# Two transformer-like layers on one core: the orders of all five queues and the PSUM banks replaced by newly searched lists

## The chip, the core and the metric

The kernel runs on one core of a Trainium2 chip. The metric is the device time of one execution in microseconds; the median of the timed executions counts. Five engines work side by side, each through a queue of its own in order: TensorE (PE, with its weight loads PEld), VectorE (DVE), ScalarE (ACT), GpSimd (POOL) and SyncE (SP), which here issues all DMAs.

## The reference

Two layers, each a sliding-window attention block and an MLP block on x of 2048 tokens by 576:

```python
def _A_ref(x, wqkv, wo):
    H = 32; Dh = D // H; W = 256
    q, k, v = heads(x @ wqkv)                      # 32 heads of 18
    scores = einsum("bhqd,bhkd->bhqk", q, k) * Dh ** -0.5
    scores = where(0 <= i - j < W, scores, -1e9)   # causal, the last 256 tokens
    return merge(einsum("bhqk,bhkd->bhqd", softmax(scores), v)) @ wo

def _B_ref(x, w1, b1, w2, b2):
    h = gelu(layernorm(x) @ w1 + b1)               # 576 -> 4608
    return h @ w2 + b2

x = x + _A_ref(layernorm(x), wqkv, wo)
x = x + _B_ref(layernorm(x), w1, b1, w2, b2)
x = x + _A_ref(layernorm(x), wqkv, wo)             # the same weights again
x = x + _B_ref(layernorm(x), w1, b1, w2, b2)
```

## The kernel before

The tokens are cut into four chunks of 512 (four tiles of 128), so two layers give eight chunks, numbered 0 to 7 here; 4 to 7 are the second layer. x stays in SBUF in float32. The weights of the MLP don't fit and are streamed again for every chunk.

A chunk passes through these stages. *Normalization*: VectorE's statistics, GpSimd's root, VectorE's scaled copy, and a DMA transpose that SyncE issues. *Queries, keys and values* (`qkv`): per tile six products of 288 columns; VectorE or ScalarE copies them out of PSUM, and a DMA transpose brings queries and keys into the layout for the scores (stage names such as q1.3: chunk 1, tile 3). *Attention* (`E`): the heads form eight groups. For each group TensorE computes scores (`scores` for chunks 0, 1 and 4, `halves` with tiles of 64 columns for the others), ScalarE takes the exponential (`exps`, L978), GpSimd cuts the band's edges (`cut`, L987), and TensorE multiplies with the values (`pv`, L1058; stage names such as ea6.p0); VectorE transposes and normalizes the result. Part a, b and c of a chunk's attention run beside the MLP of the chunk before. *Tail*: the output projection (L1182), the residual, the next normalization. *MLP* in three thirds: an up product with GELU (`G_part`, L1227 and L1237; stages ga, gb, gc) and a down product (`mm2`; stages ma, mb, mc) that adds to the residual through VectorE (L1164).

How TensorE's tasks are built matters for the change. A task is a run of matmuls that is not interrupted, and it has a *mode*, the tiling of the array: "f" whole array, "r" and "q" scores in tiles of 32 rows, "c" tiles of 32 columns, "h" two halves of 64 rows. In mode "h" (the up product, the output projection, and queries, keys and values from chunk 2 on) a product is two tasks on the same two banks: the second one (`own=True`) adds what the other half of the array contributes, and waits until the first has ended. The products in mode "c" can be *narrow* (four matmuls of 32 columns, L843) or *wide* (one of 128 columns, L840), with the same result. `schedule` decides which: where the planner's clock finds that 300 instructions would pass within 5.4 us (`dense`, constants FETCH and FETCH_US), a run of such products is made wide.

The order of the work is written out. The builder makes 4077 tasks with numbers, and `ORDER` lists for each of the five queues the numbers in the order in which that queue runs them; `BANKS` gives the PSUM bank (one of eight) of each of 1149 allocations, in the order of the task numbers. Semaphore waits follow from what tasks read and write. `schedule` runs a planner's clock over the lists with each task's cost only to decide wide or narrow and to put filler matmuls into early gaps. So `"... 768 769 466 ..."` in TensorE's list means: both halves of a product of chunk 2's first tile, then the first scores of chunk 1.

Task numbers used below: 782 to 811 products of chunk 2's tiles (stage q2); 374, 377 product and transpose of the last query tile of chunk 1, 382 the transpose of its last key tile, 466 the scores that need them; 235 and 240 pieces of wo, 328 the broadcast of b2; 413 to 450, 814 to 851, 1341 to 1378, 1868 to 1905, 2301 to 2327 output projections; 1300 to 1341 and 1812 to 1865 products of chunks 3 and 4; 1517, 3124, 3509 products with the values, 3520 scores.

## Time and profile before

| | us |
|---|---|
| median of three timed executions | 861.28 (860.0 to 861.43) |
| profiled execution, its own time | 858.9 |
| span of the profiled execution | 857.2 |
| TensorE busy in it | 843.1 |
| ScalarE busy | 611.2 |
| VectorE busy | 391.0 |
| GpSimd busy | 371.7 |

The span is what the trace covers; 1.7 us lie around it. Matmuls are pipelined and the profile models their ends, so a busy TensorE can contain pauses: they show when the starts of neighbouring rows are compared. A row of the timeline reads: start, length, engine, line, operation, tile written and tiles read, shape, count, and in brackets the idle time before it with what released it. "issue" stands for time in which an engine waited for nothing that the profile shows.

### The profile page before, as it was taken

Reading aid. Unit: us, or ns where it says so; the run is one execution under the profiler, and the core shown is the slowest. Engines: PE = TensorE matmul, PEld = TensorE weight load, DVE = VectorE, ACT = ScalarE, POOL = GpSimd, SP = SyncE. Lnnn points to the kernel's source line nnn. Section 1 sums busy time; section 2 is a strip of 40 time slices with the busy share of each in tenths; the row PEclk is TensorE's granted clock in tenths of the full one; section 3 lists DMA queues with packets and bytes.
Section 4 is the critical chain, followed back from the end, with each engine's and each line's share of the span. In section 5 each row is a group of like instructions: output and inputs, shape, how many; then the busy total and the mean of one; then the engine's idle time right before and its main releaser. Section 6 shows DMA issues by size and latency. Waiting matters only on the chain.

```text
span 857.2 us, 28905 instructions
## 1 busy us (share of the span) xinstructions
PE 843.1 (98%) x12490; PEld 525.2 (61%) x12490; DVE 391.0 (46%) x943; ACT 611.2 (71%) x1052; POOL 371.7 (43%) x551
## 2 busy tenths in 40 slices
PE   9999999999999999999999999999999999999998
PEld 6555655656656566665576665756656666656656
DVE  7877324654228442474354633564224624253103
ACT  5888886878867788488715898548887689962550
POOL 4766734545234644256500493415544266331100
DMA  9796746354475634936277545485527753636510
GB/s 226 128 153 112 219 115 176 79 152 113 141 162 95 176 113 132 192 49 160 88 226 159 116 100 141 93 196 124 169 95 194 159 140 107 206 130 180 184 68 28
DMA packets 181999, 119.91 MB, mean 140 GB/s; under 512 B 107504, under 2 KB 181872, under 8 KB 181872
## 3 DMA queue, kind: packets, MB, share of 16 engines
q1 hardware_dynamic: 181872, 118.05, 55.8%
q8 instruction: 99, 1.62, 0.8%
q14 instruction: 28, 0.23, 0.1%
HBM read 90.10 MB, written 2.36 MB: 108 GB/s over the span
## 4 chain that ended last, share of the span: by engine, by line
PE 93%; ACT 2%; DVE 2%; issue 1%; DMA 1%; POOL 1%; SPq 0%; DVEq 0%
PE ps L1227 33%; PE ps L840 28%; PE ps L905 8%; PE ps L843 7%; PE ps L1058 5%; PE ps L1182 4%; PE ps L1037 4%; PE ps L1002 2%; ACT pT L978 2%; PE ps L859 2%; DMA kT<-qn 1%; POOL pT L987 1%; PE ps L741 0%; DVE oq L1064 0%; DVE xn L780 0%
## 5 line engine op out<-in xcount | busy, mean ns | idle before, releaser
L978 ACT ACTIVATE pT<-ps 128x512 bf16<-128x512 f32 (+5 forms) x692 | 363.7, 638 | 59.6 <-PE ps L1037 38.2
L987 POOL TENSOR_SCALAR_AFFINE_SELECT pT<-pT 128x512 bf16<-128x512 bf16 (+1 forms) x360 | 278.7, 798 | 218.9 <-ACT pT L978 217.4
L1227 PE MATMUL ps<-xnTm,w_sb 64*128 64x512 bf16 x2592 | 293.2, 376 | 1.3 <-DVE x_res L1164 0.4
L1237 ACT ACTIVATE hT<-ps,b1col 128x512 bf16<-128x512 f32 x276 | 169.7, 689 | 145.9 <-PE ps L1227 144.8
L840 PE MATMUL ps<-w_sb,hT 128*128 128x288 bf16 x1674 | 220.0, 287 | 0.8 <-issue 0.7
L1227 PEld LDWEIGHTS ps<-xnTm,w_sb 64*128 64x128 bf16 x2592 | 130.0, 94 | 139.7 <-issue 7.2
L840 PEld LDWEIGHTS ps<-w_sb,hT 128*128 128x128 bf16 x1674 | 156.3, 98 | 52.5 <-issue 11.1
L1164 DVE TENSOR_TENSOR x_res<-ps,x_res 128x288 f32<-128x288 f32 x224 | 98.9, 451 | 187.9 <-PE ps L840 141.2
L905 PE MATMUL ps<-wqkv,xnTa 64*128 64x288 bf16 x1296 | 93.8, 283 | 0.9 <-ACT pT L978 0.2
L885 DVE CAST qn<-ps 128x288 bf16<-128x288 f32 x104 | 44.0, 450 | 106.8 <-PE ps L905 102.1
L905 PEld LDWEIGHTS ps<-wqkv,xnTa 64*128 64x128 bf16 x1296 | 62.5, 94 | 29.8 <-PE ps L905 4.1
L1064 DVE STREAM_TRANSPOSE oq<-ps 128x512 f32<-128x512 f32 x64 | 45.7, 714 | 69.6 <-PE ps L1058 68.8
L764 POOL TENSOR_SCALAR vtmp<-mv_all 128x1 f32<-128x1 f32 (+1 forms) x43 | 10.0, 233 | 147.9 <-DVE mv_all L755 145.8
L843 PE MATMUL ps<-w_sb,hT 128*32 128x288 bf16 x1752 | 61.1, 287 | 0.0
L1242 POOL TENSOR_TENSOR x_res<-x_res,b2bc 128x576 f32<-128x576 f32 x32 | 40.6, 1283 | 34.0 <-ACT hT L1237 33.8
L751 DVE BATCH_NORM_STATS2 st_all<-x_res 128x6 f32<-128x288 f32 (+1 forms) x128 | 52.7, 444 | 3.6 <-DMA x_res<-in_A_x_dram 3.4
L1058 PE MATMUL ps<-pT,vA 128*20 128x384 bf16 (+2 forms) x1440 | 50.9, 273 | 1.6 <-issue 1.3
L885 DVE CAST vA<-ps 128x288 bf16<-128x288 f32 x56 | 24.0, 448 | 60.0 <-PE ps L905 59.3
L843 PEld LDWEIGHTS ps<-w_sb,hT 128*32 128x32 bf16 x1752 | 44.1, 97 | 10.8 <-issue 3.9
L1037 PE MATMUL ps<-qT,kT 32*64 32x256 bf16 (+4 forms) x2080 | 42.7, 252 | 0.8 <-ACT pT L978 0.8
L1182 PE MATMUL ps<-wo_sb,attT 64*128 64x288 bf16 x576 | 42.0, 283 | 0.8
L1058 PEld LDWEIGHTS ps<-pT,vA 128*20 128x20 bf16 x1440 | 29.1, 91 | 18.5 <-issue 5.9
(62 smaller groups left out, 483.6 us busy)
## 6 DMA issues: line engine op xcount, KB each, us to landing
w_sb<-in_B_w_dram SPq DMA_DIRECT2D x46, 864.0 KB, 5.9
w_sb<-in_B_w_dram SPq DMA_DIRECT2D x48, 768.0 KB, 5.4
w_sb<-in_B_w_dram SPq DMA_DIRECT2D x96, 48.0 KB, 3.5
out_dram<-x_res SPq DMA_DIRECT2D x16, 144.0 KB, 2.8
wqkv<-in_A_wqkv_dram SPq DMA_DIRECT2D x3, 576.0 KB, 5.5
x_res<-in_A_x_dram SPq DMA_DIRECT2D x3, 576.0 KB, 4.4
wqkv<-in_B_w_dram SPq DMA_DIRECT2D x2, 864.0 KB, 8.5
wo_sb<-in_A_wo_dram SPq DMA_DIRECT2D x4, 144.0 KB, 2.9
```

Of the source, the lines that this page charges most:

```text
L840: return e.matmul(bank(b)[:, 0:HB], lhs, rhs, start=start, stop=stop, skip_group_check=True)
L843: ins = e.matmul(bank(b)[32 * j:32 * j + 32, 0:HB], lhs[:, 32 * j:32 * j + 32], rhs, start=start, stop=stop, tile_position=(0, 32 * j), sk ...
L885: return e.tensor_copy(dst, src)
L905: ins = e.matmul(bank(bs[o])[:, 0:HB], xnTa[r:r + 64, c, i * 128:(i + 1) * 128], wqkv[r:r + 64, c, col:col + HB], start=(c == 4), stop=(ph ...
L978: add("act", lambda e, h2=h2: e.activation(pT[:, sl, 2 * h2:2 * h2 + 2, dst:dst + n], two(bs[h2])[:, :, src:src + n], ACT.Exp, scale=SCALE ...
L987: add("pool", lambda e: e.affine_select(ap, ap, pattern=pat, compare_op=(ALU.is_ge if kind == "d" else ALU.is_gt), fill=0.0, base=0, chann ...
L1037: ins = e.matmul(two(bs[j // 2])[64 * u:64 * u + 64, j % 2, 64 * col:64 * (col + n)], k_of(T0 + so)[0][32 * j:32 * j + 32, g, 64 * u:64 * ...
L1058: ins = e.matmul(bank(bo)[32 * j:32 * j + VW, qo * 128:(qo + nq) * 128], vA[:, (T0 + so) % VS, 8 * j + g, :], pT[:, sl, j, col:col + nq * ...
L1164: add("dve", lambda e: e.tensor_tensor(x_res[:, t, sl], bank(b)[:, 0:HB], x_old[:, t, sl], ALU.add), reads=[b] + ([f"xin{t}"] if first els ...
L1182: ins = e.matmul(bank(bs[o])[:, 0:HB], attT[r:r + 64, c, i * 128:(i + 1) * 128], wo_sb[r:r + 64, c, o * HB:o * HB + HB], start=(c == 4), s ...
L1227: ins = e.matmul(bank(bks[i])[:, 0:n], w1_sb[r:r + 64, sls[i], col:col + 128], xnTm[r:r + 64, k % 2, c, 0:n], start=(c == 4), stop=(ph == ...
L1237: add("act", lambda e, ff=ff, hd=hd, bk=bk: e.activation(hd[:, 0:n], bank(bk)[:, 0:n], ACT.Gelu_apprx_tanh, bias=b1col[:, ff:ff + 1]), rea ...
```

## The change

The five lists of `ORDER` and the string `BANKS` are replaced: 945 of 1175 places of TensorE's list hold another task, 872 of 1055 of ScalarE's, 784 of 943 of VectorE's, 453 of 547 of GpSimd's, 305 of 357 of SyncE's, and 982 of 1149 bank numbers differ. The tasks are the same. The planner's cost of a `halves` task falls by 0.02 us (HALF_EXTRA), and its costs for VectorE's and ScalarE's copies of the first chunk's products rise to 0.435 and 0.42 us. The lists' lines that the prediction speaks of, and the rest of the diff:

```diff
 PACE = {"f": 16.0, "c": 65.0, "r": 100.0, "h": 18.5, "s": 33.0, "q": 160.0}
-HALF_EXTRA = 0.05
+HALF_EXTRA = 0.03
 FETCH = 300
...
 ORDER = {
     "pe":
...
-        "247 336 384 257 342 227 262 341 266 359 369 252 373 275 374 271 294 360 378 284 379 279 299 365 364 289 370 303 308 "
-        "782 783 758 312 759 772 777 773 778 461 316 768 769 466 763 764 425 426 471 413 414 449 476 450 437 438 485 791 481 "
...
-        "1840 1841 1689 1517 1617 1690 1686 1521 1687 1674 1671 1528 1672 1680 1681 1677 1626 1678 1538 1633 1675 1683 1684 "
...
-        "3163 3004 3096 3159 3171 3015 3172 3160 3153 3154 3105 3168 3169 3025 3112 3165 3166 3150 3128 3151 3124 3135 3186 "
...
-        "3576 3591 3566 3578 3567-3569 3590 3592 3476 3655 3497 3667 3668 3656 3673 3513 3674 3520 3509 3658 3659 3601 3661 "
...
+        "247 331 257 384 227 262 341 342 266 359 252 360 271 275 379 369 284 364 294 373 279 299 365 378 289 370 374 308 312 "
+        "758 782 759 303 783 772 777 773 778 461 316 768 769 466 763 329 764 425 426 471 413 414 449 476 450 437 438 485 786 "
...
+        "1505 1845 1840 1846 1841 1517 1617 1689 1690 1686 1521 1674 1687 1528 1675 1671 1672 1626 1680 1677 1681 1538 1633 "
...
+        "3015 3154 3159 3160 3105 3171 3172 3168 3025 3112 3165 3169 3166 3124 3128 3305 3310 3306 3311 3186 3135 3177 3188 "
...
+        "3569 3566 3578 3568 3579 3590 3592 3476 3497 3655 3667 3668 3656 3673 3513 3674 3658 3520 3509 3659 3676 3601 3661 "
...
     "sp":
...
-        "242 324 325 237 245 403 232 354 236 363 377 368 235 240 328 382 762 767 409 412 424 436 460 448 719 579 578 540 541 "
...
+        "238 235 233 349 403 363 406 368 243 382 377 232 240 781 762 246 767 409 412 245 436 460 424 448 719 328 539 578 540 "
...
 BANKS = (
-        "076102773623254242404063044624420401540205741676503072304020214204145376776476745031236203530030333603112726025527"
...
 
 
 def build_kernel(nc, A_x, A_wqkv, A_wo, B_x, B_w1, B_b1, B_w2, B_b2, out):
@@ -912,7 +912,7 @@
                 for o in range(2):
                     add("dve", lambda e, o=o, b=bs[o]: drain(e, vA[:, sv, o * 16:(o + 1) * 16, 0:DH],
                                                            bank(b)[:, 0:HB].rearrange("p (h d) -> p h d", d=DH)),
-                        reads=[bs[o]] + scale, writes=[f"v{sv}h{o}"], cost=0.375, lat=0.14, prio=prio)
+                        reads=[bs[o]] + scale, writes=[f"v{sv}h{o}"], cost=0.375 if k else 0.435, lat=0.14, prio=prio)
             else:
                 sl = qn_ctr[0] % NQN
                 qn_ctr[0] += 1
@@ -921,10 +921,10 @@
                     dst = qv[:, 2 * o:2 * o + 2, :, 0:DH]
                     if o == 1 and (k == 0 and i < 3 or k == 2):
                         add("act", lambda e, b=bs[o], dst=dst: e.copy(dst, heads_of(bank(b))) if k else e.mul(dst, heads_of(bank(b)), rstd[:, i:i + 1]),
-                            reads=[bs[o]] + scale, writes=[f"qn{sl}h{o}"], cost=0.32, lat=0.17, prio=prio)
+                            reads=[bs[o]] + scale, writes=[f"qn{sl}h{o}"], cost=0.32 if k else 0.42, lat=0.17, prio=prio)
                     else:
                         add("dve", lambda e, b=bs[o], dst=dst: drain(e, dst, heads_of(bank(b))),
-                            reads=[bs[o]] + scale, writes=[f"qn{sl}h{o}"], cost=0.375, lat=0.14, prio=prio)
+                            reads=[bs[o]] + scale, writes=[f"qn{sl}h{o}"], cost=0.375 if k else 0.435, lat=0.14, prio=prio)
                 if w == "q":
                     qd, qname = q_of(k)
                     dst, dn = qd[:, :, i * 128:(i + 1) * 128], f"{qname}{i}"
```

More of the change, by code (lines that the diff above doesn't have):

```diff
@@ new lines @@
+        "012345677601345206065670147043657323553263411630020420353056240650440326602606502450032005024026127625477226754477"
+        "775243572437243423605057033630763360270525601210364452502202506502063647744775367420101230346060461630127204563765"
+        "210761054652552101025765476544325670243150205062052560404244064667742743327364136270505040261313132723707053405126"
+        "726350205520026466327477154106032476571206757717610321045012313046724463664236004464231416520601725424532016701460"
@@ L568, in build_kernel @@
+        "506337176237664243773045675326335736362102457561010470404247053570335022040677267726227563401275430630562050753227"
+        "465563747230101422626664267154001066241520424230170673512450663460375761212673075211204350157263561740670131334264"
+        "504762564")
 def build_kernel(nc, A_x, A_wqkv, A_wo, B_x, B_w1, B_b1, B_w2, B_b2, out):
```

14 lines of the change are left out of this document (4 added, 10 removed), and 324 rows, old and new, of the table ORDER.

## The prediction

> **What bounds the kernel now.** I read the page first, then the waits of TensorE, then the chain of waits in order of time, then TensorE's timeline at the places that the chain and the waits point to.
>
> From the page: span, busy times, the chain's shares by engine, the two groups that stand between scores and their product with the values, and the queue that brings instructions.
>
> ```profile
> span 857.2 us, 28905 instructions
> PE 843.1 (98%) x12490; PEld 525.2 (61%) x12490; DVE 391.0 (46%) x943; ACT 611.2 (71%) x1052; POOL 371.7 (43%) x551
> ...
> q8 instruction: 99, 1.62, 0.8%
> ...
> PE 93%; ACT 2%; DVE 2%; issue 1%; DMA 1%; POOL 1%; SPq 0%; DVEq 0%
> ...
> L978 ACT ACTIVATE pT<-ps 128x512 bf16<-128x512 f32 (+5 forms) x692 | 363.7, 638 | 59.6 <-PE ps L1037 38.2
> L987 POOL TENSOR_SCALAR_AFFINE_SELECT pT<-pT 128x512 bf16<-128x512 bf16 (+1 forms) x360 | 278.7, 798 | 218.9 <-ACT pT L978 217.4
> ```
>
> TensorE is 93% of the chain. No arithmetic is taken away by the change, so the gain can lie only in TensorE's idle time, 857.2 - 843.1 = 14.1 us, and in pauses inside what counts as busy. The waits of TensorE (total, times, longest):
>
> ```profile
> PE ps L731 <- DVE warm L725: 1.6, 1, 1.6
> PE ps L1002 <- DMA kT<-qn: 1.3, 1, 1.3
> PE ps L1058 <- issue: 1.3, 2, 1.0
> PE ps L1037 <- ACT pT L978: 0.8, 2, 0.5
> PE ps L1002 <- ACT pT L978: 0.8, 4, 0.2
> PE ps L840 <- issue: 0.7, 1, 0.7
> PE ps L1227 <- DVE x_res L1164: 0.4, 1, 0.4
> ```
>
> From the chain of waits in order of time (start, us, what):
>
> ```profile
> 159.66 2.31 PE ps L840 x18
> ...
> 166.91 2.33 PE ps L843 x72
> ...
> 710.94 2.42 ACT pT L978 x6
> 713.42 2.04 POOL pT L987 x3
> ...
> 830.70 23.64 PE ps L840 x192
> ```
>
> The last row ends at 854.34, so 2.9 us of the idle time are the way out of the last tile, and the first 1.6 us are the wait for the zeroed tile. Neither step changes: the first four and the last stage's tasks are of the same kinds in both orders. That leaves 14.1 - 2.9 - 1.6 = 9.6 us of idle time inside. A wide matmul costs 23.64 / 192 = 0.123 us in a long run. Eighteen wide matmuls take 2.31 us and the same work in 72 narrow ones 2.33, so which products are narrow costs nothing by itself. Following the planner's rule over the new order I count 330 wide down products instead of 329.
>
> **The change part by part.** No operation is added or removed. The cost constants (HALF_EXTRA and the three drains of the first chunk) only feed the planner's clock, which decides wide or narrow and the filler matmuls at the start; I cost them at nothing. What runs differently is the order of each queue and the banks.
>
> First, *pairs of halves*. The products of queries, keys and values from the third chunk on, the output projection and the MLP's first product run as two half tasks into the same two banks, and the second half waits for the first to be finished. TensorE's timeline where the halves follow each other directly (third chunk's projection, two tiles, one score task, two tiles) and where other halves stand between them (sixth chunk's, three tiles):
>
> ```profile
> 261.81 2.86 PE L1182 MATMUL ps<-wo_sb,attT 64*128 64x288 bf16 x36
> 264.60 0.42 PE L1037 MATMUL ps<-qT,kT 32*64 32x320 bf16 x16
> 264.95 2.92 PE L1182 MATMUL ps<-wo_sb,attT 64*128 64x288 bf16 x36
> 267.80 0.40 PE L1037 MATMUL ps<-qT,kT 32*64 32x256 bf16 x16
> ...
> 556.43 3.47 PE L1182 MATMUL ps<-wo_sb,attT 64*128 64x288 bf16 x54
> 559.74 1.24 PE L1227 MATMUL ps<-xnTm,w_sb 64*128 64x512 bf16 x10
> ```
>
> Between starts, three interleaved tiles take 559.74 - 556.43 = 3.31 us, 1.10 a tile. Two tiles with adjacent halves take 2.79 and 2.85. Less 2.20 and one change of array mode (0.09, below) that is 0.25 to 0.28 us a pair; I take 0.25. Such adjacent pairs are counted in the two lists: 23 before. Twelve of them are parted (782/783, 763/764, 800/801, 805/806, 850/851, 1304/1305, 1309/1310, 1313/1314, 1840/1841, 1868/1869, 2301/2302, 2791/2792) and three are new (791/792, 814/815, 826/827), so 14 after. 9 x 0.25 = **-2.2 us**. What hides each is the task put between, of at least 0.27 us. Ends: -2.3, and -1.1 if half of them only uncover another wait.
>
> Second, *changes of array mode*.
>
> ```profile
> 586.10 2.38 PE L840 MATMUL ps<-w_sb,hT 128*128 128x288 bf16 x18
> 588.40 0.43 PE L1037 MATMUL ps<-qT,kT 32*64 32x320 bf16 x24
> ```
>
> Eighteen wide matmuls and the change to scores take 588.40 - 586.10 = 2.30; 18 x 0.123 = 2.21, so a change costs about 0.09 us. With each task's mode the lists have 376 changes before and 372 after: **-0.4 us**.
>
> Third, *the transposed keys of the second chunk*. SyncE's timeline (its issues wait in order), then TensorE's, then what the tile kT's answer says of landing:
>
> ```profile
> 50.68 3.01 SPq L948 DMA_TRANSPOSE x_res<-qn  x2
> 53.79 1.29 SPq L948 DMA_TRANSPOSE kT<-qn  x1
> 55.12 1.06 SPq L691 DMA_DIRECT2D wo_sb<-in_A_wo_dram  x2
> 56.22 0.42 SPq L691 DMA_DIRECT2D b2bc<-in_B_b_dram  x1
> 56.69 1.24 SPq L948 DMA_TRANSPOSE kT<-qn  x1
> ```
>
> ```profile
> 62.98 0.34 PE L1002 MATMUL ps<-x_res,xnTm 32*128 32x384 bf16 x4 [1.31 <-DMA kT<-qn]
> ```
>
> ```profile
> DMA to landing us min/median/max: 3.1/4.6/6.0
> ```
>
> The last key transpose (task 382) is issued at 56.69, behind two pieces of wo and the broadcast of b2, and task 466 (62.98) waits 1.31 us for it. In the new SyncE order these three no longer stand before it (235 goes ahead of the transposes, 240 and 328 go behind), which frees 56.69 - 55.12 = 1.6 us: the issue comes at about 55.1. The last query transpose (377) now follows it, at about 56.4; with the median landing of 4.6 it is there at 61.0, with the largest at 62.4. TensorE arrives at 62.98 - 1.31 = 61.7. Task 374, which feeds 377, becomes the last product of its chunk, about 6 us later by the tasks that pass it; 377's issue was the second of the row at 50.68, so that estimate still leaves it time. The wait becomes 0 to 0.7: I take **-1.0 us**; ends -1.3 and +0.7 (it lands as late as the largest, behind a queue that is 1.3 us slower).
>
> Fourth, *dense places*. Three of the waits have nothing that released them ("issue", 2.0 us together):
>
> ```profile
> 299.27 0.55 PE L1058 MATMUL ps<-pT,vA 128*20 128x384 bf16 x9
> 300.85 0.61 PE L1058 MATMUL ps<-pT,vA 128*20 128x384 bf16 x15 [1.03 <-issue]
> ...
> 649.83 1.39 PE L840 MATMUL ps<-w_sb,hT 128*128 128x288 bf16 x10 [0.69 <-issue]
> ```
>
> They stop TensorE in the middle of a task, behind narrow products, scores and products with the values, which bring most instructions per us; the page's instruction queue moved 99 blocks of 16 KB. I read them as instructions that came late. With starts instead of modelled ends they cost about 2.8 us. Laying both lists out with the durations above, 38 tasks before and 27 after begin a stretch of 2 us with over 140 matmuls and weight loads, but the densest such stretch has 160 in both. 2.8 x 11/38 = **-0.8**; I take -0.7; ends -2.8 (all gone) and +2.0 (as many more: where a block is late is partly chance).
>
> A rule speaks against this part: the Trainium skill's page "Runtime: NRT & Kernel Launch", section "Instruction fetch mechanics", says that fetching in blocks of 256 instructions runs ahead and is hidden by the issue rate. The block size agrees with 99 blocks for some 25,000 instructions; the three waits do not agree with "hidden". By that rule this term is 0 and the sum -2.8.
>
> Fifth, *other waits*. Two known ones lose their place: the 0.4 us for L1164 at the fourth chunk's up product (2063 moves back by over 5 us of work) and the one at 714.89,
>
> ```profile
> 714.89 0.43 PE L1037 MATMUL ps<-qT,kT 32*64 32x320 bf16 x24 [0.47 <-ACT pT L978]
> 715.50 0.73 PE L1058 MATMUL ps<-pT,vA 128*20 128x384 bf16 x20 [0.18 <-POOL pT L987]
> ```
>
> where a further down-product task (3658, 6 x 0.123 = 0.74 us) now stands before the scores 3520. Against that, two products with the values come nearer to their scores: 3124 has three down-product tasks before it (2.2 us) and 1517 four halves (2.3), while two exponentials and one cut take 2 x 0.64 + 0.80 = 2.1 us by the page's means, without the ways between them. I put 0.9 gained against 0.9 there, and **+0.8** for waits of the same kind that I cannot see in a list. Ends -3 and +5.
>
> Sum: -2.2 - 0.4 - 1.0 - 0.7 + 0.8 = -3.5 us. The profiled execution took 858.9 us (span 857.2 and 1.7 around it), so the same execution would take 855.4. It lies 2.4 under the median of the timed runs, 861.28; the forecast for that is 861.28 - 3.5 = **857.8 us**. A measurement of this kernel can tell 0.2%, 1.7 us, from no change.
>
> **The rivals.** *Late cuts* (slower): a product with the values waits for exponentials on ScalarE and the cut on GpSimd, because both queues were reordered too. The place at 710.94 to 715.5 shows the mechanism, with 2.42 us of exponentials and 2.04 of cuts on the chain and 0.47 + 0.18 = 0.65 us of TensorE idle. With ten more such places among the 64 products, 6.5 - 3.5 = +3.0: 864.3. It decides against the forecast from six places and is slower by over 0.2% from nine. For it speaks that ScalarE is 71% busy and that the shortest stretches shrink; against it, that GpSimd is 43% busy and the seven largest waits hold only this one place of the kind after the start. *As many waits as before*: what is parted in one place meets in another, and only the mode changes and half of the pairs remain, -0.4 - 1.1, less than can be told: 859.8; for it speaks that the densest stretch did not change. *The dense places are really gone*: -2.8 instead of -0.7: 855.7. *The price buys nothing there*, because instructions come in time and the three waits have another cause: -0.7 falls away: 858.5. The fetch section of the Trainium skill named above speaks for this one. *The keys stay late*: -1.0 falls away: 858.8.
>
> **How the numbers follow.** Forecast with the keys late or the fetch term at 0 (857.8 to 858.8): 0.50. Dense places gone: 0.12. As many waits as before: 0.24. Late cuts: 0.14. Faster 0.50 + 0.12 = 0.62, same 0.24, slower 0.14. The forecast's own range is 855.7 to 859.5. The wide one reaches down to the pairs, keys and dense ends with some of the other waits (-7.3: 854.0) and up through the middle case to seven or eight late cuts (7.5 x 0.65 - 3.5 = +1.4: 862.7); it leaves out 0.06 below and 0.12 above.
>
> **What would show it.** Right: L905's busy and idle time together fall by about 2 us, as its adjacent pairs go from ten to two; the wait of L1002 for kT is under 0.7; idle time of TensorE is about 11 to 12 us. The dense term is right if "issue" waits sum to 1 to 1.7 us, wrong at 2 or more. Late cuts would show as more waits of L1058 for L987 like the 0.18 us at 715.50. The forecast is wrong if the waits for ScalarE and GpSimd together grow by over 3 us, or if a weight or a transpose lands late and one DMA wait of over 2 us appears.

## The result and the profile after

The changed kernel takes **855.91 us** (median of 4 runs, 855.70 to 856.66) against 860.64 us for the kernel before (4 runs, 859.24 to 861.43). The ratio is **0.9948, 95% interval [0.9931, 0.9966]**: faster by 0.5%, some 4.5 us. The forecast was 857.8 us in a range of 854.0 to 862.7. The profiled execution took 856.66 us, against 858.9 before. Its page: span, busy times, the instruction queue, the chain by engine, the two groups between scores and values, and two of the groups whose products come in halves.

```profile
span 855.0 us, 28829 instructions
...
PE 840.6 (98%) x12466; PEld 527.6 (62%) x12466; DVE 390.4 (46%) x943; ACT 612.8 (72%) x1053; POOL 373.0 (44%) x551
...
q8 instruction: 98, 1.61, 0.8%
...
PE 93%; ACT 3%; issue 1%; DVE 1%; DMA 1%; POOL 1%; SPq 0%; DVEq 0%
...
L978 ACT ACTIVATE pT<-ps 128x512 bf16<-128x512 f32 (+5 forms) x692 | 363.8, 639 | 62.6 <-PE ps L1037 42.3
L987 POOL TENSOR_SCALAR_AFFINE_SELECT pT<-pT 128x512 bf16<-128x512 bf16 (+1 forms) x360 | 279.5, 802 | 251.0 <-ACT pT L978 249.8
...
L905 PE MATMUL ps<-wqkv,xnTa 64*128 64x288 bf16 x1296 | 91.7, 283 | 0.5 <-ACT qn L923 0.2
...
L1182 PE MATMUL ps<-wo_sb,attT 64*128 64x288 bf16 x576 | 42.7, 283 | 0.8
```

TensorE's busy time fell from 843.1 to 840.6 us, although no product was taken away: what went is pauses inside "busy". Its idle time did not fall: 855.0 - 840.6 = 14.4 us, against 14.1. ScalarE and GpSimd spend what they spent. The waits of TensorE (total, times, longest):

```profile
PE ps L1037 <- issue: 1.8, 2, 1.0
PE ps L1002 <- ACT pT L978: 1.3, 6, 0.3
PE ps L797 <- DVE xn L777: 1.1, 1, 1.1
PE ps L731 <- DVE warm L725: 1.0, 1, 1.0
PE ps L1058 <- issue: 1.0, 2, 0.7
PE ps L1227 <- DVE vA L885: 0.8, 1, 0.8
```

The wait of L1002 for the transposed keys is gone from the list. The waits with no releaser ("issue") are not: 2.0 us before, 2.8 after. The profile's start also shows what nobody ordered: with the same issue times at the start, the weights of the first products landed later, and L797 waited 1.1 us for a tile; that wait is 0.2 us in the second execution below, and between nothing and 1.2 us in the variants.

To place the differences I took each TensorE task's time from its first instruction to the next task's first one, less the median of its kind in the trace of before, less 0.097 us for a change of array mode. The excess is sorted into *halves* (the next task writes the same two banks), *inside* (the longest pause lies within the task: late instructions, and about 1.0 us of other small pauses, as the run with light loads below shows) and *between* (all other waits):

```
us of excess      before  after  again  rejoin  part  allwide  light  keys  fewer  p12   m72   m108  old12
halves             5.41    3.25   3.26   6.54   0.23   3.25    3.25   3.25  3.25   3.25  3.25  3.25  5.41
inside             3.96    4.88   4.83   5.28   3.50   1.87    1.01   2.69  3.57   2.48  3.37  4.17  2.91
between           11.31   11.60  10.06  11.20  18.42  14.04   10.20  10.02 13.63   9.88 10.92 10.10 12.03
adjacent halves      23      14     14     28      1     14      14     14    14     14    14    14    23
```

Before to after: halves -2.2, inside +0.9, between +0.3, together -0.9 of the -2.2 us between the two spans. The other -1.3 us lie outside the three classes: TensorE's first instruction starts at 1.0 us instead of 1.6 (-0.6), four changes of mode fewer (-0.4), and -0.3 that I can't place. The halves are the largest term, and the others nearly cancel.

### The profile page after: what moved, and what is told of

The parts are those of the page before. It is cut to its first block, busy times and chain, and to the rows that moved or that the text cites. A ratio compares the mean times of both kernels' runs of the same rounds, so it can differ in the third digit from the quotient of the medians.

```text
span 855.0 us, 28829 instructions
## 1 busy us (share of the span) xinstructions
PE 840.6 (98%) x12466; PEld 527.6 (62%) x12466; DVE 390.4 (46%) x943; ACT 612.8 (72%) x1053; POOL 373.0 (44%) x551
## 4 chain that ended last, share of the span: by engine, by line
PE 93%; ACT 3%; issue 1%; DVE 1%; DMA 1%; POOL 1%; SPq 0%; DVEq 0%
PE ps L1227 33%; PE ps L840 28%; PE ps L905 9%; PE ps L843 6%; PE ps L1058 5%; PE ps L1182 5%; PE ps L1037 4%; ACT pT L978 3%; PE ps L1002 2%; PE ps L859 1%; DMA x_res<-in_A_x_dram 1%; POOL pT L987 1%; SPq L691 0%; DVE vA L885 0%; DVE st_all L751 0%
## 5 line engine op out<-in xcount | busy, mean ns | idle before, releaser
L1227 PE MATMUL ps<-xnTm,w_sb 64*128 64x512 bf16 x2592 | 292.0, 376 | 1.7 <-DVE vA L885 0.8
L840 PE MATMUL ps<-w_sb,hT 128*128 128x288 bf16 x1692 | 221.8, 287 | 0.0
L1227 PEld LDWEIGHTS ps<-xnTm,w_sb 64*128 64x128 bf16 x2592 | 130.2, 94 | 140.3 <-issue 6.7
L840 PEld LDWEIGHTS ps<-w_sb,hT 128*128 128x128 bf16 x1692 | 158.5, 98 | 50.3 <-issue 7.1
L1164 DVE TENSOR_TENSOR x_res<-ps,x_res 128x288 f32<-128x288 f32 x224 | 99.5, 452 | 166.1 <-PE ps L840 132.5
L905 PE MATMUL ps<-wqkv,xnTa 64*128 64x288 bf16 x1296 | 91.7, 283 | 0.5 <-ACT qn L923 0.2
L905 PEld LDWEIGHTS ps<-wqkv,xnTa 64*128 64x128 bf16 x1296 | 64.2, 94 | 24.8 <-issue 2.2
L843 PE MATMUL ps<-w_sb,hT 128*32 128x288 bf16 x1680 | 57.6, 287 | 0.0
L1037 PE MATMUL ps<-qT,kT 32*64 32x256 bf16 (+4 forms) x2080 | 43.4, 253 | 2.1 <-issue 1.8
L780 DVE TENSOR_SCALAR xn<-x_res,mv_all,rstd 128x576 bf16<-128x576 f32 (+1 forms) x60 | 34.4, 584 | 12.7 <-POOL rstd L766 3.7
```

Of the source, the lines that this page charges most:

```text
L840: return e.matmul(bank(b)[:, 0:HB], lhs, rhs, start=start, stop=stop, skip_group_check=True)
L843: ins = e.matmul(bank(b)[32 * j:32 * j + 32, 0:HB], lhs[:, 32 * j:32 * j + 32], rhs, start=start, stop=stop, tile_position=(0, 32 * j), sk ...
L905: ins = e.matmul(bank(bs[o])[:, 0:HB], xnTa[r:r + 64, c, i * 128:(i + 1) * 128], wqkv[r:r + 64, c, col:col + HB], start=(c == 4), stop=(ph ...
L1037: ins = e.matmul(two(bs[j // 2])[64 * u:64 * u + 64, j % 2, 64 * col:64 * (col + n)], k_of(T0 + so)[0][32 * j:32 * j + 32, g, 64 * u:64 * ...
L1164: add("dve", lambda e: e.tensor_tensor(x_res[:, t, sl], bank(b)[:, 0:HB], x_old[:, t, sl], ALU.add), reads=[b] + ([f"xin{t}"] if first els ...
L1227: ins = e.matmul(bank(bks[i])[:, 0:n], w1_sb[r:r + 64, sls[i], col:col + 128], xnTm[r:r + 64, k % 2, c, 0:n], start=(c == 4), stop=(ph == ...
```

## The experiments

Each kernel is the changed one with the edit shown, unless it says otherwise. Times are medians; the ratio is to the kernel before, run on the same chip in the same hour. Where a difference between two variants matters, I compare their ratios or their profiled executions.

**again** is the changed kernel itself.

> The changed kernel as it is, a second time, for the share that an execution's luck has. Theory 1 (the loads at the start and the instruction blocks land at times that differ from run to run): in its profile the first weights land up to 1 us earlier or later than in the first one (7.58 us for wqA there, 6.81 before the change), the waits without a releaser come at partly other places and sum to 2 to 4 us, and the time against the kernel before is a ratio of 0.994 to 0.996. Rival (both are fixed by the order): the same landing within 0.2 us, the same places, the same sum of 2.8 us.

855.36 us (6 runs, 855.09 to 856.60), ratio 0.9956 [0.9941, 0.9970]. The result stands. The profiled execution (855.30) is 1.4 us faster than the first one (856.66): the weights at the start landed sooner (the first 12 us have 0.98 us of excess instead of 2.11). The "issue" waits are the same, 1.8 and 1.0 us, and three of the four stalls stand at the same places (229, 609 and 644 us), though each is 0.3 us longer or shorter; the smallest, at 547 us, is gone. So the landing differs from run to run, as the first theory said, and the places of the waits mostly do not, as the rival said. From here on, variants are held against this one.

**rejoin** puts the parted halves together again; everything else is as after the change.

> The changed kernel with the second halves of the twelve parted products put directly behind their first halves again (28 adjacent pairs instead of 14, 371 changes of mode instead of 372). Theory 1 (an adjacent pair costs its 0.24 us wherever it stands): 14 x 0.24 = 3.3 us slower than the changed kernel, so within 1.5 us of the kernel before. Rival (the pause only takes the place of another wait, or gives slack back to ScalarE and the DMAs): under 1 us slower than the changed kernel. L905's busy and idle time rises by about 3 us under theory 1.

```
- 758 782 759 303 783 772 ... 466 763 329 764 425 ... 510 800 796 801 797 490 805 810 806 811 505
+ 758 782 783 759 303 772 ... 466 763 764 329 425 ... 510 800 801 796 797 490 805 806 810 811 505
- 1300 1150 1295 1304 1296 1305 990 ... 1505 1845 1840 1846 1841 1517 ... 2544 2786 2791 2787 2444 2465 2792
+ 1300 1150 1295 1304 1305 1296 990 ... 1505 1845 1840 1841 1846 1517 ... 2544 2786 2791 2792 2787 2444 2465
```

859.62 us (12 runs), ratio 1.0004 [0.9990, 1.0017]. Against the 0.9956 of the run again, that is 0.0048 of 859 us, some 4.1 us slower, and as slow as the kernel before. It goes further than back, though. Putting 800/801 and 805/806 together also closes 796/797 and 810/811 up, so the trace has 28 adjacent pairs instead of 14 (the kernel before has 23), and each of the 14 costs 0.23 to 0.24 us, 3.29 in all. The group row of the projections shows it without any sorting (busy, mean | idle before):

```profile
L905 PE MATMUL ps<-wqkv,xnTa 64*128 64x288 bf16 x1296 | 93.1, 283 | 1.4 <-DVE qn L885 0.3
```

Busy and idle are 94.5 us, against 92.2 after the change and 94.7 before. The profiled executions lie 4.5 us apart; the rest is waits between tasks (+1.1) and inside them (+0.5). So parting the halves pays: going from 23 pairs to 14 is 9 x 0.235 = 2.1 us, about half of the change's 4.5. The five pairs that rejoin has more than the kernel before, and the waits, make the rest of its loss.

**part** goes the other way: the halves that the change left adjacent are parted too.

> The changed kernel with 13 of its 14 remaining adjacent pairs parted too, in the tails of the first four chunks and at three products (768, 791, 1892); banks and all other queues as they are; 373 changes of mode instead of 372. Theory 1: 13 x 0.24 - 0.1 = 3.0 us faster than the changed kernel, and L1182's busy time falls by about 2 us. Rival (the first halves that now start earlier wait for VectorE to free their banks, and the tails' time is set by the chain behind them): no gain, with new waits of L1182 for L1164.

```
- 316 768 769 466 ... 764 425 426 471 413 414 449 ... 791 792 510 ... 1341 1342 1353 1354 ... 1892 1893 1967
+ 768 316 769 466 ... 764 425 413 426 471 414 449 ... 791 510 792 ... 1341 1353 1342 1354 ... 1892 1967 1893
```

859.90 us (12 runs), ratio 1.0006 [0.9995, 1.0017]: 4.3 us slower than again by the ratios, although the halves' excess falls by 3.0. (The planner also put nine filler matmuls more in.) Waits for banks take the place of it (the group of the output projection's product, then rows of TensorE's waits):

```profile
L1182 PE MATMUL ps<-wo_sb,attT 64*128 64x288 bf16 x576 | 42.0, 283 | 3.0 <-DVE x_res L1164 1.1
```

```profile
PE ps L1037 <- DVE x_res L1164: 1.3, 2, 0.7
...
PE ps L1182 <- DVE x_res L1164: 1.1, 2, 0.8
PE ps L1002 <- DVE x_res L1164: 1.1, 2, 0.5
...
PE ps L1182 <- DVE vA L885: 0.9, 1, 0.9
```

The task that is put between takes banks that VectorE has not drained yet. The pairs that stayed adjacent stand where no other bank is free in time, so parting pays only as far as the banks allow.

**allwide** makes every down product wide, so that TensorE's program has 11,086 matmuls instead of 12,466.

> The changed kernel with every product of mode c wide (408 instead of 330, 11,086 matmuls instead of 12,466). Theory 1 (waits without a releaser are instructions that come late where many are needed): these waits fall from 2.8 us of idle time to under 1, worth 2 to 3.5 us, while 44 more changes between wide products and products with the values cost 44 x 0.095 = 4.2: 0.5 to 2 us slower than the changed kernel. Rival (they have nothing to do with the number of instructions): the waits stay at 2 to 4 us and the kernel is 4 us slower.

```
-                if lo < hi and (not at or sum(...) > 1.0 and any(dense(n) for n in range(lo, hi))):
+                if lo < hi:
```

854.87 us (6 runs), ratio 0.9949 [0.9935, 0.9963], within what can be told of again; the first theory had it 0.5 to 2 us slower. Yet much moved: no "issue" wait at all is left in its list (inside 4.83 to 1.87), and 88 blocks of instructions come instead of 98. What was gained there went to the places where a wide product stands next to a product with the values: 12 of them in the changed kernel, 56 here, at 0.10 us each (37 of one direction 3.85 us, 19 of the other 1.92), +4.5. The prediction said that "which products are narrow costs nothing by itself"; that holds beside scores, which change the mode either way, and not beside products with the values. So the waits with no releaser depend on how many instructions there are, which is what the planner's rule for narrow products works on.

**light** keeps TensorE's program and takes away transfers.

> The changed kernel with less weight traffic: from the fourth w1 slice on only a quarter of each is loaded, and from the second w2 tile on only a sixth, so later chunks of the MLP multiply by stale weights (that part of the result is not the reference's); the instructions of TensorE and all orders stay. Theory 1 (an instruction block is late only where TensorE's stretch is dense and the sixteen DMA engines are full with weights at the same time): TensorE's waits with no releaser ("issue") fall from 2.8 us of idle time to under 1, and the time falls by 2 to 4 us against the changed kernel, to about 0.991 to 0.993 of the kernel before. Theory 2 (dense places alone make blocks late): "issue" waits stay at 2 to 4 us and the time within 1 us of the changed kernel (0.9945 to 0.9965).

```
-  dma("sp", w1_sb[:, sl, 0:4 * GW]..., B_w1[0:512, cols]...
+  nc_ = 4 if B < NB1 else 1
+  dma("sp", w1_sb[:, sl, 0:nc_ * GW]..., B_w1[0:nc_ * P, cols]...
-  dma("sp", wt[:, WB * b:WB * b + WB, :], B_w2[f0 * P:(f0 + WB) * P, :]...
+  nw = WB if wn == "w2x" or k + hf == 0 and not w2n[0] else 1
+  dma("sp", wt[:, WB * b:WB * b + nw, :], B_w2[f0 * P:(f0 + nw) * P, :]...
```

851.25 us (4 runs), ratio 0.9901 [0.9884, 0.9917]. The two traces over the same 700 us (busy time of each engine with instructions, granted clock, share of the DMA engines' time, GB/s), the changed kernel first and then this one:

```profile
100.00:800.00 700.00, 695.26 (x10770) 436.24 (x10763) 307.02 (x732) 518.62 (x922) 308.49 (x442) 1.00 0.56 141
```

```profile
100.00:800.00 700.00, 698.17 (x10773) 439.30 (x10766) 307.42 (x734) 517.58 (x921) 306.88 (x441) 1.00 0.31 62
```

Same matmuls, the same number of instruction blocks, as dense as before, and no "issue" wait is left: the waits inside tasks fall by 3.8 us, to 1.01, while those between stay (10.20 against 10.06), and the profiled execution is 4.0 us faster (851.33 against 855.30). So the transfers matter: with less weight traffic none of the same dense stretches made a block late. That a block is late only while the DMA engines are full is not shown, and allnarrow (next) and m72 have waits without it.

**allnarrow** makes every down product narrow (18,358 matmuls).

> The changed kernel with every down product as 72 narrow matmuls instead of 18 wide ones (18,358 matmuls instead of 12,466; the arithmetic of TensorE's columns is the same, and changes of array mode become about 12 fewer, -1.1 us). Theory 1 (late instruction blocks cost time wherever instructions are dense): about 140 blocks instead of 98, "issue" waits of 6 us or more in all, and the time 4 to 15 us above the changed kernel, 1.000 to 1.012 of the kernel before. Theory 2 (only the stretches of scores and value products are dense enough, narrow down products alone are not): "issue" waits stay at 2 to 4 us, and the time is within 2 us of the changed kernel, 0.993 to 0.997.

```
-                if lo < hi and (not at or sum(...) > 1.0 and any(dense(n) for n in range(lo, hi))):
+                if False:
```

901.96 us (6 runs, 896.53 to 906.66), ratio 1.0486 [1.0457, 1.0516]: +46 us, three times the upper end of what the first theory gave. The blocks and TensorE's first waits:

```profile
q8 instruction: 144, 2.36, 1.1%
```

```profile
PE ps L843 <- issue: 12.2, 12, 2.5
PE ps L1058 <- issue: 6.1, 6, 2.3
PE ps L1037 <- issue: 6.1, 4, 2.6
PE ps L1227 <- DMA xnTm<-xn: 2.8, 2, 2.1
```

With 47% more blocks the waits for instructions go from 2.8 to 24.4 us of idle time. They grow much faster than the count. They are about half of the loss: the profiled execution, the fastest of the six, is 41.2 us above that of again, 21.6 of it in these waits. TensorE's busy time rose by 12.7 us (853.5 against 840.8), at a mean granted clock of 0.992 instead of 1.000, which alone would be some 7 us (an estimate: 0.8% of 853). Full DMA engines are not needed for such a wait: the block of one of them began to come at 748.2 us, after 4 us in which nothing else was transferred (the DMA share is the last figure but one):

```profile
744.20:746.20 2.00, 2.00 (x88) 1.48 (x80) 0.60 (x2) 2.00 (x5) 0.95 (x2) 1.00 0.00 0
746.20:748.20 2.00, 2.00 (x84) 1.53 (x76) 1.06 (x3) 2.00 (x6) 1.38 (x3) 1.00 0.00 0
```

```profile
750.83 1.26 PE L843 MATMUL ps<-w_sb,hT 128*32 128x288 bf16 x33 [0.47 <-issue]
```

**fewer** raises the constant of the planner's rule, so that 53 products stay narrow instead of 78 and all those near the four stalls become wide.

> The changed kernel with one constant of the planner's rule for narrow products raised (FETCH_US 5.4 to 6.6): 355 wide down products instead of 330, 53 narrow instead of 78, and among those made wide are all that lie near the four places where TensorE waited with no releaser; 12 more changes of array mode (1.1 us). Theory 1 (those waits are late instruction blocks, and fewer instructions there remove them): "issue" waits under 1 us instead of 2.8, and 1 to 2 us less time than the changed kernel, 0.9925 to 0.9945 of the kernel before. Theory 2 (the borders of blocks shift and other places are late instead): "issue" waits stay at 2 to 3 us, and the time is 0 to 1.5 us above the changed kernel, 0.9955 to 0.9975.

```
-FETCH_US = 5.4
+FETCH_US = 6.6
```

856.26 us (8 runs), ratio 0.9967 [0.9954, 0.9980]: no faster than the changed kernel. The stalls at 230, 611 and 646 us are gone, and one of 1.7 us has come at 550 us, in the middle of a *wide* product (the top row of its waits is "PE ps L840 <- issue"). As the second theory said, the late block moved. The twelve added changes cost their part.

**keys** puts SyncE's order at the key transposes of the second chunk back to the old one.

> The changed kernel with only SyncE's order at the key transposes of the second chunk put back: the last key transpose (382) goes again behind the two pieces of wo, the broadcast and the query transpose (377). Theory 1 (the wait of 466 is set by when 382 is issued): the issue comes 2 to 2.5 us later, at about 59.6 us, the landing at about 64.8, and 466 waits 1.3 to 2.3 us; the time is 1 to 2 us above the changed kernel, 0.9965 to 0.9985 of the kernel before. Theory 2 (it is set by TensorE's own arrival and by the transfers under way, since in the changed kernel the issue came at 57.15 us, later than the 56.69 before, and yet the wait was gone): 466 waits under 0.6 us, and the time is within 0.5 us of the changed kernel.

```
- 238 235 233 349 403 363 406 368 243 382 377 232 240 781 ... 719 328 539
+ 238 233 349 403 363 406 368 243 377 232 235 240 328 382 781 ... 719 539
```

853.84 us (5 runs), ratio 0.9933 [0.9919, 0.9947]: 2.0 us below again by the ratios, which neither theory had, though the two intervals overlap a little. TensorE's timeline at task 466 in the changed kernel and in this one:

```profile
61.91 1.52 PE L905 MATMUL ps<-wqkv,xnTa 64*128 64x288 bf16 x18
63.62 0.34 PE L1002 MATMUL ps<-x_res,xnTm 32*128 32x384 bf16 x4 [0.20 <-DVE attq L1070]
```

```profile
61.51 1.52 PE L905 MATMUL ps<-wqkv,xnTa 64*128 64x288 bf16 x18
62.96 0.83 PE L741 MATMUL ps<-warm 128*128 128x256 bf16 x6
63.72 0.34 PE L1002 MATMUL ps<-x_res,xnTm 32*128 32x384 bf16 x4
```

The planner saw the keys later and put six filler matmuls in front of 466. From the projection before it to 466 are 2.21 us instead of 1.71, so the old key order costs at most about 0.5 us here, fillers included, not 1.3 to 2.3: the issue did come later (58.85 us; 57.15 and 55.10 in the two executions of the changed kernel), but the transposes landed after 3.8 us at most, where the largest was 5.2 (3.8 in the second). The gain lies elsewhere: of the stalls at 230, 547, 611 and 646 us, the last two are gone ("inside" 2.69 instead of 4.83). The only thing that differs for TensorE there is that six matmuls, twelve instructions with their weight loads, have been added 550 us earlier. This made a new theory: whether a block is late depends on where its border falls.

**p12** tests that with nothing else changed: six fillers more among the first ones, where TensorE waits for data anyway.

> The changed kernel, all orders as they are, with six short filler matmuls more among the zero products of the first 7 us, where TensorE waits for the first transposes and weights anyway. Every later instruction of TensorE comes 12 places later against the borders of its blocks of 256, as in the kernel with the old key order, whose planner added six fillers. Theory 1 (whether a block is late depends on where its border falls in a dense stretch): the waits at 611 and 646 us go again, as there; "issue" idle time is 0.7 to 1.5 us instead of 2.8, and the time is 1 to 2 us below the changed kernel, 0.992 to 0.9945 of the kernel before. Theory 2 (those two waits went because SyncE's order was another): they stay, "issue" is 2.4 to 3.2 us, and the time is within 0.7 us of the changed kernel.

```
             ins = e.matmul(bank(bk)[:, 0:256], warm[:, :], ...)
+        for _ in range(6 if n == 7 else 0):
+            ins = e.matmul(bank(bk)[:, 0:P], warm[:, :], warm[:, :], start=True, stop=True)
```

**853.24 us** (6 runs, 852.66 to 855.07), ratio 0.9921 [0.9905, 0.9937], some 2.3 us below the changed kernel's first ratio and 3.0 below that of again. The stall at 611 us in the changed kernel, then the same tasks here, whose lines have moved by two:

```profile
608.81 0.42 PE L1037 MATMUL ps<-qT,kT 32*64 32x256 bf16 x16
609.16 1.65 PE L843 MATMUL ps<-w_sb,hT 128*32 128x288 bf16 x48
610.68 0.72 PE L1058 MATMUL ps<-pT,vA 128*20 128x384 bf16 x18
612.09 0.39 PE L1058 MATMUL ps<-pT,vA 128*20 128x256 bf16 x6 [0.69 <-issue]
```

```profile
607.36 0.42 PE L1039 MATMUL ps<-qT,kT 32*64 32x256 bf16 x16
607.71 1.65 PE L845 MATMUL ps<-w_sb,hT 128*32 128x288 bf16 x48
609.23 0.83 PE L1060 MATMUL ps<-pT,vA 128*20 128x384 bf16 x24
609.99 0.43 PE L1039 MATMUL ps<-qT,kT 32*64 32x320 bf16 x24
```

The same products run without a break. In the changed kernel the block's transfer began at 609.71 us and ended at 610.67, and in the 2 us before it the DMA engines were full (the share is the last figure but one; the rows are the stalls at 611, 646, 230 and 547 us in this order):

```profile
607.70:609.70 2.00, 1.89 (x45) 1.22 (x46) 1.23 (x3) 2.00 (x7) 0.30 (x1) 1.00 0.98 342
643.00:645.00 2.00, 2.00 (x92) 1.66 (x74) 1.86 (x6) 1.93 (x6) 0.00 (x0) 1.00 0.96 339
227.20:229.20 2.00, 2.00 (x88) 1.66 (x76) 1.69 (x4) 1.99 (x5) 0.00 (x0) 1.00 1.02 369
543.10:545.10 2.00, 2.00 (x52) 1.35 (x53) 0.46 (x1) 1.93 (x7) 1.81 (x3) 1.00 1.06 344
```

With the border twelve instructions off, the blocks of 611 and 646 us came at 605.22 and 640.19 us, 2 to 3 us earlier by TensorE's work (2.5 us ahead of the narrow product that begins at 607.71, where the other came 0.55 behind it). The 2 us before these two blocks:

```profile
603.20:605.20 2.00, 2.00 (x36) 1.67 (x30) 0.34 (x1) 1.98 (x3) 0.00 (x0) 1.00 1.07 394
638.20:640.20 2.00, 2.00 (x36) 1.48 (x32) 0.28 (x1) 1.98 (x3) 0.00 (x0) 1.00 0.26 71
```

The first came while the engines were full and yet in time, the second while they were hardly used. The traces show directly that these waits are blocks that came late. I numbered TensorE's instructions (matmuls, weight loads, semaphore events) in all fourteen traces. After the first 20 us, 48 pauses inside a task are over 0.35 us longer than the task's usual spacing, in twelve of the traces. In every one of them the first late instruction is number 193 modulo 256, and TensorE goes on 2.2 to 2.8 us after the start of a transfer on the instruction queue. So all of them stand at a border between blocks.

The n-th transfer begins near the n-th of these borders, mostly after it, and a wait at the next border ends 2.2 to 2.8 us after that start. How long after its border the transfer begins, its lag, is what differs: from the tenth block on it is over 2 us for 23 of 88 blocks in both executions of the changed kernel, and for 3 of 88 in light. At the stalls at 611 and 646 us the lag is 3.6 and 2.3 us (3.9 and 2.6 in the second execution), while the instructions of the block before take 5.0 and 3.4 us: 3.6 + 2.4 - 5.0 is the pause of 1.0. In p12 the lags there are 1.0 and 0.4 us, and nothing waits.

Twelve instructions are only some 0.2 us of TensorE's work there. Why they change the lag by 2 to 3 us no run shows; that the block's transfer then comes ahead of a burst of weights and not behind it would fit. What is left is 0.71 us at 229 and 0.41 at 545. The shift accounts for the gain that came with the old key order. And since p12 has the new key order and keys the old one, with the same fillers in number, the 1.0 us between their ratios is another bound for the key order, though the intervals overlap.

**m72** and **m108** shift the borders the other way, by 72 and by 108 instructions, through products that run before all four places.

> The changed kernel with the two narrow down-product tasks 1159 and 1160 (202.4 and 203.2 us) made wide: 36 matmuls fewer, so that every later instruction of TensorE comes 72 places earlier against the borders of its blocks; two changes of array mode more (0.2 us). All of the four places where TensorE waited for its instructions are later and stay as they are. Theory 1 (borders decide): of the four waits (1.0, 0.6, 1.0 and 1.2 us by starts) at least two change by over 0.4 us, or new ones come at other dense places; the time differs from the changed kernel by the difference in their sum, anything from -3 to +2 us. Theory 2 (the place decides, wherever the borders fall): all four stay within 0.4 us, and the time is within 0.7 us of the changed kernel.

> As the kernel with 1159 and 1160 wide, but with the three narrow tasks 1026, 1034 and 1035 (167.0 to 168.5 us) wide instead: 54 matmuls fewer, a shift of 108 places against the blocks of 256, two changes of array mode more (0.2 us). Theory 1 (borders decide): the waits differ from those of the changed kernel and from those of the shift by 72, in at least two of the four places by over 0.4 us, with the time following their sum (-3 to +2 us). Theory 2 (the place decides): all four stay within 0.4 us, the time within 0.7 us.

```
+        for st, t in pe:
+            if t.idx in (1159, 1160):
+                t.wide[0] = True
```

In m108 the tasks in brackets are 1026, 1034 and 1035. m72 takes 854.88 us (6 runs), ratio 0.9940 [0.9924, 0.9957]; m108 **853.01 us** (6 runs, 851.94 to 854.47), ratio 0.9913 [0.9896, 0.9929]. The stalls: when the task in which each falls starts, and its size by starts (again is added for what differs between two executions of one kernel):

```
after   230.4 1.04   546.5 0.55   610.7 0.97   646.0 1.20                sum 3.76
again   229.4 0.76   -            608.7 1.31   644.4 1.48                sum 3.55
p12     229.3 0.71   545.2 0.41   -            -                             1.12
m72     -            547.4 1.02   -            -           713.1 0.88        1.90
m108    -            548.0 1.93   -            -           500.6 1.12        3.05
```

A dash stands for less than 0.35 us. All four change in both: three are gone, and the one at 547 us falls in another task. Between the two executions of the changed kernel the same four differ by at most 0.4 us each. The stall of m72 at 713 us came after a lag of 2.2 us, and the DMA engines, full from 707 to 709 us (share 0.98), had gone idle before the block's transfer at 711.25:

```profile
709.25:711.25 2.00, 2.00 (x51) 1.38 (x52) 0.46 (x1) 2.00 (x5) 1.11 (x2) 1.00 0.00 1
```

```profile
714.12 0.24 PE L1040 MATMUL ps<-qT,kT 32*64 32x128 bf16 x3 [0.65 <-issue]
```

The largest in m108:

```profile
547.95 0.53 PE L846 MATMUL ps<-w_sb,hT 128*32 128x288 bf16 x9
550.24 2.02 PE L846 MATMUL ps<-w_sb,hT 128*32 128x288 bf16 x60 [1.76 <-issue]
```

The profiled execution of m108 is the slowest of its six. Its median lies 1.5 us under it, so executions of one kernel differ by as much as the stalls do. That m108 has the lowest median is therefore not explained by its trace. Its interval lies wholly below both intervals of the changed kernel, so it beats both kernels; p12 is next, and its interval lies below that of again and overlaps the first one a little.

**old12** is the kernel *before* with the six fillers.

> The kernel before, all its orders as they were, with the same six short filler matmuls among the zero products of the first 7 us: every later instruction of TensorE comes 12 places later against the borders of its blocks (up to 0.4 us may be paid for the fillers at the start, where TensorE waits less than in the changed kernel). Theory 1 (the waits with no releaser in the old order, 1.4, 0.6 and 0.9 us by starts at 299, 591 and 649 us, depend on the borders like those of the new one): at least two of the three change by over 0.3 us or new ones come, and the time differs from the kernel before by their sum. Theory 2 (they belong to the old order's dense places, wherever the borders fall, and only the new order's are a matter of borders): all three stay within 0.3 us and the time is 0 to 0.5 us above the kernel before, 1.000 to 1.001.

859.30 us (12 runs), ratio 0.9998 [0.9986, 1.0010]. The time is the same, but not the stalls: those at 299 and 591 us (1.4 and 0.6 by starts) are gone, the one at 649 has grown from 0.87 to 1.68, and one of 0.78 has come at 559. TensorE's timeline at the grown one:

```profile
647.58 0.43 PE L1039 MATMUL ps<-qT,kT 32*64 32x256 bf16 x21
649.47 0.22 PE L1039 MATMUL ps<-qT,kT 32*64 32x64 bf16 x3 [1.46 <-issue]
```

The old order's stalls are a matter of borders too. The two "issue" waits in its list make 1.5 + 0.6 = 2.1 us, against 2.0 without the fillers.

## Why the prediction was right, and where it was not

The sign, the size and the main term held: -3.5 us was forecast, 0.9948 is -4.5 in the runs, and the profiled executions differ by -2.2 (858.9 to 856.66) and by -3.6 with the second one (855.30). By the forecast's own reckoning the profiled one should have taken 855.4. That the second one meets it is partly luck: the dense places missed by 1.6 us, and this was made up elsewhere. The waits between tasks, with the first instruction that starts 0.6 us earlier, came to -1.85 us where the keys and the other waits together were put at -0.2; no run tells why. One sign of being right failed: TensorE's idle time was to be 11 to 12 us, and it is 14.4, and 12.7 in the second execution.

- **Pairs of halves, -2.2.** Right in number and cause. The sorted trace gives 5.41 - 3.25 = -2.16, and rejoin measures 0.235 us a pair. The row of L905 falls by 2.5 us of busy and idle time together (94.7 to 92.2), where about 2 was said to show it. The end of -1.1, half the pairs only uncovering another wait, was not seen: rejoin loses them all.
- **Changes of array mode, -0.4.** The count stands, but the list of modes left out that a wide product beside a product with the values is a change as well, at 0.10 us: 10 such places before, 12 after, so about -0.2 remains.
- **Transposed keys, -1.0.** The number was met: the wait of 466 is gone, and the excess of 57 to 64 us goes from 1.88 to 0.46, and to 0.96 in the second execution. The reason holds in part. The last key transpose was issued at 57.15 us in the first execution, where all of the start ran later, and at 55.10 in the second, just as forecast; in neither did 466 wait for it. So those 2 us didn't matter. Putting SyncE's order back costs at most about 0.5 us. Part of the 1.31 us belonged to that one execution: in old12, with the old order, the same scores wait 0.58 us, which the profile puts down to ScalarE. What the rest of the gain there came from is open. The first row is the issue in again, the second the wait in old12:

```profile
55.10 1.24 SPq L948 DMA_TRANSPOSE kT<-qn  x1
```

```profile
63.30 0.34 PE L1004 MATMUL ps<-x_res,xnTm 32*128 32x384 bf16 x4 [0.58 <-ACT attq L1077]
```

- **Dense places, -0.7.** This term failed, in sign and in reason. The "issue" waits went from 2.0 to 2.8 us of idle time (by starts 2.84 to 3.76, +0.9); "wrong at 2 or more" was the mark. The step that failed is "2.8 x 11/38": it let the number of dense stretches set the waits. The reading of the waits as late instructions was right (allwide, and the 48 pauses that all stand at a block's border), but in a dense stretch it is the lag of the block's transfer that decides, and this changes with the traffic (light) and with where the border falls (p12, m72, m108). In five kernels with the new order and its borders in four positions (the changed one, keys, p12, m72, m108) the lists' "issue" waits sum to 0.7 to 2.8 us, and in two positions of the old order to 2.0 and 2.1. With so few positions, whether the new order is better or worse in this respect stays open. The rule that was weighed there, in the Trainium skill's page "Runtime: NRT & Kernel Launch", section "Instruction fetch mechanics", that fetching is mostly hidden, agrees with light and fails in allnarrow, where it leaves 24.4 us uncovered, and at four places of the changed kernel.
- **Other waits, +0.8.** In the first execution the class "between" rose by 0.3 with the keys' -1.4 in it, so others rose by 1.7. The first 12 us alone make 1.9 of that, by loads that landed later, and only 0.8 in the second execution. I wrote that the wait for the zeroed tile would not change; it fell from 1.6 to 1.0 us, and gave nothing, because the first product of the weights started at 8.06 us (7.91 in the second execution) instead of 7.54. The two waits that were to lose their place did: L1037 after 714 us has none now, and no wait of L1227 for L1164 stands near 385 us.
- **Late cuts**, the slower rival, did not come: the waits for ScalarE sum to 1.9 us in the list of after, against 2.5 before, and none for GpSimd is in it (0.2 before), although ScalarE's and GpSimd's queues were reordered as much.
- **The base.** The forecast subtracts from 861.28, the median of three runs. Twenty-three later runs of the same kernel have a median of 858.88. The difference is as large as a term of the sum, and only ratios within one call are free of it.

## What to carry to other kernels

Look for tasks that follow each other into the same banks: here each costs 0.24 us, can be counted from the list, and is won by one independent task between them, as long as its own banks are free. When waits without a releaser stand in a trace of many small instructions, count blocks, see whether the waits stand at the blocks' borders, look at the DMA share before them, and run the kernel with its borders shifted by a few fillers before judging any order by them: here twelve instructions were worth at least half as much as the whole new order. Judge a reordering of some us from two executions at least, and from ratios to a kernel run beside it.

## What the runs showed of the hardware

- A block of TensorE's instructions can be late by 0.4 to 1.9 us in the middle of a task (2.6 us of idle time in allnarrow). With the same instructions and less weight traffic (DMA share 0.56 to 0.31) it never was; with 144 blocks instead of 98 the waits grew from 2.8 to 24.4 us. In the stalls at 230, 547, 611 and 646 us the DMA share of the 2 us before was 0.96 or more; but p12 has a share of 1.07 before its block of 605.22 us and no stall there, so full engines alone are not enough; and m72 and allnarrow have stalls with a share of 0.00 in the 2 us before, so they are not needed either.
- The 48 pauses of this kind in twelve traces all stand at instruction 193 modulo 256 of TensorE's queue, and end 2.2 to 2.8 us after the start of a transfer on the instruction queue.
- Between a wide product and a product with the values, TensorE loses 0.10 us, as between a wide product and scores.
- The same program, with the same issue times, got its first weights about 1 us later in one execution than in another (median landing of the three 576 KB loads of wqkv 6.5 and 5.3 us), and TensorE followed.
